# Transposes by DMA in place of a trip through DRAM, and whole tables in place of placed ones, in a spectral filter with a feed-forward layer on one core

## The chip, the cores and the metric

One core of one Trainium2 chip (trn2). The metric is the device time of one execution in microseconds, lower is better. Most executions of a kernel agree within 0.3%. Verdicts compare a kernel with the kernel before on the same chip, in the same rounds.

In the profile lines PE is TensorE's matmuls and PEld its weight loads, DVE is VectorE, ACT ScalarE, POOL GpSimd; SPq and ACTq are the queues from which SyncE and ScalarE issue DMAs; L723 is a line of the kernel. The chain that ended last is the work followed back from the last instruction, at each step to what released it. The granted clock is the share of TensorE's full clock that it was given.

## The reference, cut to what matters

```python
# x: (8, 3008, 256); w_r, w_i: (256, 256); moe_w_in: (256, 2048); moe_w_out: (2048, 256)
X = np.fft.rfft(x, axis=1)
Yr = Xr @ w_r - Xi @ w_i + b_r            # and Yi likewise
Y = soft_threshold(Yr, 0.01) + 1j * soft_threshold(Yi, 0.01)
y = np.fft.irfft(Y, n=3008, axis=1)
h = np.maximum(y.reshape(24064, 256) @ moe_w_in, 0)
out = (s * h * h + b) @ moe_w_out
```

The kernel splits the transform of length 3008 into 94 x 32. A batch goes through four stages: the first transform over 94 points (matrix A_t), the second over 32 (F_t) with the mixing by w, the inverse over 32 (T_t), and the last over 94 (C_t). Then come the two large matrix products, which fill most of TensorE's time. The stages of the next batches are woven into the large products of the present one. The plan counts in slots: one slot is a sixteenth of a tile of the large layer, some 1.08 us.

Of the kernel before, what the change touches and what calls it, by code (L numbers as in the profile page):

```python
# [9 lines left out]
F16 = mybir.dt.float16  # L10
# [4 lines left out]
P = 128  # L15
# [81 lines left out]
def kernel(  # L97
# [26 lines left out]
    F_d = nc.inline_tensor(fwd.astype(np.float16), name="dft_fwd").ap()  # L124
    T_d = nc.inline_tensor(inv.astype(np.float16), name="dft_inv").ap()
# [14 lines left out]
    upool = ctx.enter_context(tc.tile_pool(name="up", bufs=3))  # L140
    uspool = ctx.enter_context(tc.tile_pool(name="usp", bufs=5))
# [3 lines left out]
    vspool = ctx.enter_context(tc.tile_pool(name="vsp", bufs=2))  # L145
# [75 lines left out]
    F_c = uspool.tile([P, NPAIR, 2, N2], F16, name="F_c", tag="us")  # L221
# [6 lines left out]
    T_c = uspool.tile([P, NPAIR, 64], F16, name="T_c", tag="us")  # L228
# [9 lines left out]

    def emit_load_forward():
        nc.sync.dma_start(  # L240
            out=F_c[:, 0:H].rearrange("p q r k -> p q (r k)"), in_=F_d[:, 0:H]
        )
        nc.sync.dma_start(out=sel_t, in_=S_d)

    def emit_load_inverse():
        nc.sync.dma_start(
            out=F_c[:, H:].rearrange("p q r k -> p q (r k)"), in_=F_d[:, H:]
        )
        t_load = nc.sync.dma_start(out=T_c, in_=T_d)
# [22 lines left out]
    F_t = cpool.tile([P, NPAIR, P], F16, name="F_t")  # L272
    nc.vector.memset(F_t, 0.0)
    T_t = cpool.tile([P, NPAIR, P], F16, name="T_t")
    nc.vector.memset(T_t, 0.0)
    F_2 = [uspool.tile([P, H, P], F16, name="F_2", tag="us") for _ in range(2)]
    for f in F_2:
        nc.gpsimd.memset(f, 0.0)
# [21 lines left out]
    def place_f(h):  # L300
        q = slice(h * H, h * H + H)
        for a in range(2):
            r = slice(64 * a, 64 * a + 64)
            nc.scalar.copy(out=blocks(F_t)[r, q, :, a], in_=F_c[r, q])

    def place_f_2(h):

        q = slice(h * H, h * H + H)
        for a in range(2):
            r = slice(64 * a, 64 * a + 64)  # L310
            nc.vector.tensor_scalar_mul(
                out=blocks(F_2[h])[r, :, 0, a], in0=F_c[r, q, 1], scalar1=-1.0
            )
            nc.vector.tensor_copy(out=blocks(F_2[h])[r, :, 1, a], in_=F_c[r, q, 0])

    def place_t(h):
        q = slice(h * H, h * H + H)
        for i in range(4):
            r = slice(32 * i, 32 * i + 32)
            c = 64 * (i % 2)  # L320
            nc.vector.tensor_copy(out=T_t[r, q, c : c + 64], in_=T_c[r, q])
# [28 lines left out]
    def first_batch():  # L350
# [3 lines left out]
        for g in range(N2 // 4):  # L354
# [26 lines left out]
            if c == 2:  # L381
                with tc.issue_after(last_dve.ins):
                    nc.vector.memset(F_c[0:1, H, 0, 0:1], 0.0)
                    nc.vector.memset(T_c[0:1, 0, 0:1], 0.0)
# [4 lines left out]
        with tc.issue_after(last_dve.ins), tc.issue_after(last_act.ins):  # L389
            place_f(0)  # L390
            place_f_2(0)

        gate = nc.gpsimd.tensor_copy(out=w_in_t[0][0:1, 0:1], in_=T_c[0:1, 0, 0:1])
# [9 lines left out]
        g_last = [None]  # L403

        def mix(ec, u):
# [10 lines left out]
            if u % 3 == 1:  # L416
                g_last[0] = nc.scalar.copy(out=g, in_=ps)
                load["act"] += 1.02
            else:
                g_last[0] = nc.vector.tensor_tensor(  # L420
# [47 lines left out]
        for h in range(2):  # L468
            vs[(0, h)] = vspool.tile([96, HW, D], F16, name="vs", tag="vs")

        def turn(ec, k):
            ps = two_banks()
            for j in range(8):
# [4 lines left out]
            h, n = divmod(8 * k, HW)  # L478
            evac(
                vs[(0, h)][:, n : n + 8, ec * P : (ec + 1) * P],  # L480
# [5 lines left out]
        def last_dft(ec, n2):  # L486

            ps = [one_bank(), other_bank()]
            for j in range(8):
                h, k = divmod(n2 + j, HW)  # L490
                nc.tensor.matmul(
                    ps[j // 4][:, (j % 4) * 96 : (j % 4) * 96 + 96],
                    vs[(0, h)][:, k, ec * P : (ec + 1) * P], C_t,
# [8 lines left out]
        more = s1_units(1, True)  # L502
# [7 lines left out]
        for i in range(2 * U + 2):  # L510
# [13 lines left out]
            if i == 0:  # L524
                with tc.issue_after(g_last[0].ins):
                    place_t(0)
            if i == 1:
# [397 lines left out]
```

## The kernel before: the parts that the change touches

```python
def s1_units(b, more_banks=False):                  # first stage of a batch, 16 units
    def unit(i):
        c, j = divmod(2 * i, XCH)
        ps = ...
        nc.tensor.matmul(ps[0:96, :], A_t[0:N1, :], x16[(b, c)][0:N1, j * D : (j + 2) * D], ...)
        evac(u[0:96, j : j + 2, :], ps..., 512)     # ScalarE or VectorE, by a tally
        if j == XCH - 2:                            # four stores to DRAM ...
            nc.sync.dma_start(out=ud[:, c * XCH : (c + 1) * XCH, :], in_=u[0:96])
        if i == N2 // 2 - 1:                        # ... and four loads in the other layout
            for q in range(4):
                t = ...
                nc.sync.dma_start(out=t, in_=uv[:, 6 * q : 6 * q + 6, :])

def inv_unit(i):                                    # inverse over 32 (in s23_units)
    ...
    if i % 2 == 1:                                  # v goes to DRAM, six stores a batch
        nc.sync.dma_start(out=vd[2 * i - 2 : 2 * i + 2]..., in_=v)
    if i == H - 1:                                  # after the last: vs is read back, in two loads
        for h in range(2):
            t = ...
            nc.sync.dma_start(out=t..., in_=vv[:, h * HW * D : (h + 1) * HW * D])

# s4_units: the last transform, matmuls on C_t and vs

for b in range(2, B):                               # s0, s1, s2: first slots of batches b-2, b-1, b
    p = s1 - s0
    schedule(s0 + 40, p - 48, s1_units(b))          # first stage ends 8 slots before s1
    p = s2 - s1
    schedule(s1 + 2, p - 30, s23_units(b))          # vs of batch b is requested near s2 - 28
    schedule(s2 - 14, 12, s4_units(b))              # and read from s2 - 14 on
```

SyncE issues all of these DMAs, and the stores of the output, in the order in which they stand in its instruction stream.

## Time and profile before

| | before |
|---|---|
| median of three runs | 851.42 us (851.32 to 852.76) |
| span of the profiled run | 849.4 us |
| TensorE busy | 835.0 us |
| granted clock of TensorE, mean | 0.997 |
| waits of TensorE for vs | none |

The lines behind it stand in the prediction. One reads them from the top: if TensorE is busy for 98% of the span, a change can win only by giving TensorE less to do, or in the start-up, where TensorE idles.

### The profile page before, as it was taken

The numbers are of one execution on the slowest core, as the hardware profiler recorded it, in microseconds if no ns is written. First come the engines' busy times: TensorE is split into PE (matmuls) and PEld (weight loads), VectorE is DVE, ScalarE is ACT, GpSimd is POOL, SyncE is SP. The second block draws the span as 40 slices with busy tenths as digits, with TensorE's granted clock in tenths as the row PEclk, the third lists the DMA queues.
The fourth block names the chain that finished last, engine by engine and source line by source line (L and its number), as shares of the span: only waits on it lengthen the run. The fifth ranks groups of instructions, "written<-read, shape, count | busy, mean of one in ns | idle before, by whom it ended". The sixth has DMA issues, their size and how long they took to land.

```text
span 849.4 us, 17085 instructions
## 1 busy us (share of the span) xinstructions
PE 835.0 (98%) x6645; PEld 600.5 (71%) x6645; DVE 697.0 (82%) x1027; ACT 643.2 (76%) x856; POOL 46.6 (5%) x72
## 2 busy tenths in 40 slices
PE   8899999999999999999999999999999999999997
PEld 7757777777677766777677776777667777766765
DVE  6898987888888987888878888888977888776674
ACT  5898887787778787787777887787877787766673
POOL 5321000000000000000000000000000000000000
PEclk9999999999999999999999999999999999999999
DMA  7937457324761367324662247613354223411111
GB/s 165 161 104 162 108 148 185 101 76 100 177 186 54 92 159 184 109 78 103 171 177 65 74 106 199 172 40 92 100 156 118 62 79 98 112 33 38 38 44 50
DMA packets 105458, 95.07 MB, mean 112 GB/s; under 512 B 9510, under 2 KB 97578, under 8 KB 104034
## 3 DMA queue, kind: packets, MB, share of 16 engines
q1 hardware_dynamic: 98930, 79.57, 32.6%
q0 software_dynamic: 6448, 14.42, 10.7%
q8 instruction: 52, 0.85, 0.4%
q14 instruction: 28, 0.23, 0.1%
HBM read 52.54 MB, written 46.66 MB: 117 GB/s over the span
## 4 chain that ended last, share of the span: by engine, by line
PE 88%; DVE 4%; ACT 3%; DMA 2%; issue 1%; POOL 0%; SPq 0%; DVEq 0%; ACTq 0%; POOLq 0%
PE psa L832 36%; PE psh L761 36%; PE psf L627 4%; PE psf L562 2%; PE psf L613 2%; PE psf L598 2%; PE psf L657 2%; PE psf L710 2%; ACT rt L768 1%; DVE gt L775 1%; DMA x<-in_x_dram 1%; DMA out_dram<-ost 1%; PE psh L410 1%; ACT yt L160 0%; ACT vs L160 0%
## 5 line engine op out<-in xcount | busy, mean ns | idle before, releaser
L768 ACT ACTIVATE rt<-psh 128x1024 f32<-128x1024 f32 (+2 forms) x384 | 387.1, 1009 | 119.1 <-PE psh L761 117.7
L775 DVE TENSOR_TENSOR gt<-rt 128x1024 f16<-128x1024 f32 (+2 forms) x321 | 384.0, 1199 | 98.1 <-ACT rt L768 97.4
L832 PE MATMUL psa<-w_out_t,gt 128*128 128x256 f16 (+1 forms) x3024 | 454.3, 272 | 0.1
L832 PEld LDWEIGHTS <-gt 128*128 128x128 f16 (+1 forms) x3024 | 300.9, 101 | 187.2 <-issue 1.7
L761 PE MATMUL psh<-yt,w_in 128*128 128x512 f16 (+1 forms) x1344 | 396.7, 378 | 0.3 <-ACT rt L768 0.3
L761 PEld LDWEIGHTS <-w_in 128*128 128x128 f16 x1536 | 142.9, 98 | 27.4 <-issue 2.1
L842 DVE SCALAR_TENSOR_TENSOR ost<-psa,s_bc,bias_bc 128x512 f32<-128x512 f32 (+2 forms) x97 | 71.0, 732 | 8.3 <-PE psa L832 7.1
L772 ACT ACTIVATE gt<-rt 128x1024 f16<-128x1024 f32 (+2 forms) x63 | 66.2, 1050 | 1.0
L632 DVE TENSOR_TENSOR ring<-psf,s 128x512 f16<-128x512 f32 x84 | 57.5, 684 | 3.7 <-PE psf L627 2.9
L160 ACT CAST v<-psf 128x512 f16<-128x512 f32 x78 | 45.3, 582 | 18.7 <-PE psf L657 18.7
L160 ACT CAST xf<-psf 128x512 f16<-128x512 f32 x82 | 47.9, 585 | 10.9 <-PE psf L598 10.8
L160 ACT CAST u<-psf 96x512 f16<-96x512 f32 x77 | 44.5, 580 | 11.0 <-PE psf L562 10.7
L761 PE MATMUL psh<-tail,w_in 128*128 128x512 f16 (+1 forms) x192 | 52.1, 353 | 0.0
L627 PE MATMUL psf<-W_g,xf 128*128 128x256 f16 x336 | 50.4, 273 | 0.0
L160 ACT CAST yt<-psf 128x480 f16<-128x480 f32 (+2 forms) x75 | 38.1, 520 | 13.6 <-PE psf L710 13.6
L189 POOL DMA_DIRECT2D x<-in_x_dram x36 | 18.9, 530 | 429.3 <-PE psf L562 428.0
L562 PE MATMUL psf<-x,A_t 94*96 94x512 f16 x104 | 39.7, 381 | 1.7 <-ACT yt L160 0.5
L638 DVE TENSOR_TENSOR ring<-ring,high 128x512 f16<-128x512 f16 x84 | 35.5, 423 | 2.3
L639 DVE TENSOR_TENSOR ring<-ring 128x512 f16<-128x512 f16 x84 | 35.5, 422 | 1.9
L637 DVE TENSOR_TENSOR ring<-ring,low 128x512 f16<-128x512 f16 x84 | 35.4, 421 | 1.6
L627 PEld LDWEIGHTS <-xf 128*128 128x128 f16 x336 | 32.9, 98 | 3.8
L710 PE MATMUL psf<-C_t,vs 96*128 96x96 f16 x448 | 33.0, 205 | 0.1
(89 smaller groups left out, 501.9 us busy)
## 6 DMA issues: line engine op xcount, KB each, us to landing
out_dram<-ost SPq DMA_DIRECT2D x152, 128.0 KB
ud<-u SPq DMA_DIRECT2D x28, 384.0 KB
us<-ud SPq DMA_DIRECT2D x28, 384.0 KB
vd<-v SPq DMA_DIRECT2D x42, 256.0 KB
vs<-vd SPq DMA_DIRECT2D x14, 768.0 KB
x<-in_x_dram POOLq DMA_DIRECT2D x28, 376.0 KB, 5.9
ring<-ring SPq DMA_DIRECT2D x280, 32.0 KB
out_dram<-ost SPq DMA_DIRECT2D x16, 120.0 KB
```

What stands on the lines that cost most here:

```text
L160: return None, nc.scalar.copy(out=dst, in_=src)
L562: nc.tensor.matmul(ps[0:96, :], A_t[0:N1, :], x16[(b, c)][0:N1, j * D : (j + 2) * D], start=True, stop=True,)
L627: nc.tensor.matmul(ps[:, r, :], xt[:, 2 - r, dc], W_g[:, dc, r], start=(dc == 0), stop=(dc == DC - 1),)
L632: nc.vector.tensor_tensor(out=t, in0=ps, in1=hold[i // 2][:, i % 2].unsqueeze(1).to_broadcast([P, 2, D]), op=ALU.add,)
L638: nc.vector.tensor_tensor(out=m, in0=m, in1=high, op=ALU.min)
L710: nc.tensor.matmul(ps[:, j * 96 : (j + 1) * 96], vs[(b, h)][:, k, ec * P : (ec + 1) * P], C_t, start=True, stop=True,)
L761: nc.tensor.matmul(o, w_in_t[dc][:, mc * P : (mc + 1) * P], r, start=(dc == 0), stop=(dc == DC - 1),)
L768: nc.scalar.activation(out=rt[:, :, 0:w], in_=ps[:, :, 0:w], func=AF.Relu)
L772: nc.scalar.activation(out=gt[:, :, 0:w], in_=rt[:, :, 0:w], func=AF.Square)
L775: nc.vector.tensor_tensor(out=gt[:, :, 0:w], in0=rt[:, :, 0:w], in1=rt[:, :, 0:w], op=ALU.mult)
L832: nc.tensor.matmul(ps[0:size, h, :], gts[(ti, mc // 2)][:, mc % 2, sub * size : (sub + 1) * size], w_out_t[:, mc, :], start=(mc == 0), sto ...
L842: nc.vector.scalar_tensor_tensor(out=ost[0:size, 0:k], in0=ps[0:size, 0:k], scalar=s_bc[0:size], in1=bias_bc[0:size, 0:k], op0=ALU.mult, o ...
```

## The change

The intent: the first stage's result for batches 2 to 7 no longer goes through DRAM to change its layout. TensorE computes it with the two operands exchanged, so that it lies with the 256 features on partitions, and two transposing DMAs a batch turn it, SBUF to SBUF. The stage is moved 20 slots ahead of where it ended. Besides, the inverse table and the second half of the forward tables are loaded whole, where they were spread on the chip by VectorE and ScalarE.

```diff
+        def unit_late(i):
+            ...
+            for j in range(4):
+                nc.tensor.matmul(
+                    ps[:, j * 96 : j * 96 + 96], x16[(b, c)][0:N1, lo : lo + P],
+                    A_t[0:N1, :], start=True, stop=True,
+                )
+            evac(u[:, dc, :, 4 * g : 4 * g + 4], ps[:, 0:384]..., 384)
+            if i == N2 // 2 - 1:
+                us[b] = uspool.tile([P, NPAIR, D], F16, name="us", tag="us")
+                for dc in range(DC):
+                    nc.sync.dma_start(
+                        out=us[b][:, :, dc * P : (dc + 1) * P],
+                        in_=u[:, dc].rearrange("p k n -> p (k n)"),
+                        transpose=True,
+                    )
... (batch 1 keeps the trip through DRAM)
-        schedule(s0 + 40, p - 48, s1_units(b))
+        lead = 40 if b == 2 else 28
+        schedule(s0 + lead, p - lead - 28, s1_units(b))
...
-        t_load = nc.sync.dma_start(out=T_c, in_=T_d)
+        nc.sync.dma_start(out=T_t[:, 0:H], in_=t_d[:, 0:H])
+        nc.sync.dma_start(out=F_t[:, H:], in_=f_d)
+        nc.sync.dma_start(out=F_2[1], in_=f_2_d)
+        t_load = nc.sync.dma_start(out=T_t[:, H:], in_=t_d[:, H:])
... (place_t and the second calls of place_f and place_f_2 go; us, u and vs get single buffers, each of a whole batch)
```

More of the change, by code (lines that the diff above doesn't have):

```diff
@@ L123 @@
     A_d = nc.inline_tensor(first.astype(np.float16), name="dft_first").ap()
-    F_d = nc.inline_tensor(fwd.astype(np.float16), name="dft_fwd").ap()
-    T_d = nc.inline_tensor(inv.astype(np.float16), name="dft_inv").ap()
+    F_d = nc.inline_tensor(fwd[:, 0:H].astype(np.float16), name="dft_fwd").ap()
+    f_all = np.zeros((P, NPAIR, 2, 2, N2))
+    t_all = np.zeros((P, NPAIR, 2, 64))
+    for i in range(4):
+        r = slice(32 * i, 32 * i + 32)
+        f_all[r, :, :, i // 2] = fwd.reshape(P, NPAIR, 2, N2)[r]
+        t_all[r, :, i % 2] = inv[r]
+    f_2 = np.stack([-f_all[:, H:, 1], f_all[:, H:, 0]], axis=2)
+    f_d, f_2_d, t_d = (
+        nc.inline_tensor(t.reshape(P, -1, P).astype(np.float16), name=name).ap()
+        for t, name in ((f_all[:, H:], "fwd_rest"), (f_2, "fwd_rest_i"), (t_all, "dft_inv"))
+    )
     C_d = nc.inline_tensor(last.astype(np.float16), name="dft_last").ap()
@@ L139 @@
     xpool = ctx.enter_context(tc.tile_pool(name="xp", bufs=4))
-    upool = ctx.enter_context(tc.tile_pool(name="up", bufs=3))
-    uspool = ctx.enter_context(tc.tile_pool(name="usp", bufs=5))
+    upool = ctx.enter_context(tc.tile_pool(name="up", bufs=1))
+    uspool = ctx.enter_context(tc.tile_pool(name="usp", bufs=1))
     xfpool = ctx.enter_context(tc.tile_pool(name="xfp", bufs=4))
@@ L144 @@
     vpool = ctx.enter_context(tc.tile_pool(name="vp", bufs=3))
-    vspool = ctx.enter_context(tc.tile_pool(name="vsp", bufs=2))
+    vspool = ctx.enter_context(tc.tile_pool(name="vsp", bufs=1))
     ypool = ctx.enter_context(tc.tile_pool(name="yp", bufs=2))
@@ L220 @@
             nc.sync.dma_start(out=b_g[r : r + 1, i], in_=bv.unsqueeze(0))
-    F_c = uspool.tile([P, NPAIR, 2, N2], F16, name="F_c", tag="us")
+    first_c = uspool.tile([P, 5, H * 64], F16, name="first_c", tag="us")
+    F_c = first_c[:, 0].rearrange("p (q r k) -> p q r k", q=H, r=2)
+    F_2 = [
+        first_c[:, 1 + 2 * i : 3 + 2 * i].rearrange("p s (q k) -> p (s q) k", k=P)
+        for i in range(2)
+    ]
     b_h = cpool.tile([P, D], F16, name="b_h")
@@ L227 @@
     sel_t = cpool.tile([P, P], F16, name="sel_t")
-    T_c = uspool.tile([P, NPAIR, 64], F16, name="T_c", tag="us")
     eye_t = cpool.tile([P, P], F16, name="eye_t")
@@ L237 @@
     bb_bc = cpool.tile([P, 1], F32, name="bb_bc")
+    F_t = cpool.tile([P, NPAIR, P], F16, name="F_t")
+    T_t = cpool.tile([P, NPAIR, P], F16, name="T_t")
     def emit_load_forward():
         nc.sync.dma_start(
-            out=F_c[:, 0:H].rearrange("p q r k -> p q (r k)"), in_=F_d[:, 0:H]
+            out=F_c.rearrange("p q r k -> p q (r k)"), in_=F_d
         )
@@ L245, in emit_load_inverse @@
     def emit_load_inverse():
-        nc.sync.dma_start(
-            out=F_c[:, H:].rearrange("p q r k -> p q (r k)"), in_=F_d[:, H:]
-        )
-        t_load = nc.sync.dma_start(out=T_c, in_=T_d)
+        nc.sync.dma_start(out=T_t[:, 0:H], in_=t_d[:, 0:H])
+        nc.sync.dma_start(out=F_t[:, H:], in_=f_d)
+        nc.sync.dma_start(out=F_2[1], in_=f_2_d)
+        t_load = nc.sync.dma_start(out=T_t[:, H:], in_=t_d[:, H:])
         with tc.issue_after(t_load.ins):
@@ L271 @@
     nc.vector.memset(neg_lam, -LAM)
-    F_t = cpool.tile([P, NPAIR, P], F16, name="F_t")
-    nc.vector.memset(F_t, 0.0)
-    T_t = cpool.tile([P, NPAIR, P], F16, name="T_t")
-    nc.vector.memset(T_t, 0.0)
-    F_2 = [uspool.tile([P, H, P], F16, name="F_2", tag="us") for _ in range(2)]
-    for f in F_2:
-        nc.gpsimd.memset(f, 0.0)
+    nc.vector.memset(F_t[:, 0:H], 0.0)
+    nc.gpsimd.memset(F_2[0], 0.0)
     def make_bounds():
@@ L298, in place_w, with place_f, place_f_2 @@
             nc.scalar.copy(out=W_t[:, :, i], in_=w_st[i])
-    def place_f(h):
-        q = slice(h * H, h * H + H)
+    def place_f():
         for a in range(2):
             r = slice(64 * a, 64 * a + 64)
-            nc.scalar.copy(out=blocks(F_t)[r, q, :, a], in_=F_c[r, q])
-    def place_f_2(h):
-        q = slice(h * H, h * H + H)
+            nc.scalar.copy(out=blocks(F_t)[r, 0:H, :, a], in_=F_c[r])
+    def place_f_2():
         for a in range(2):
@@ L311, in place_f_2 @@
             nc.vector.tensor_scalar_mul(
-                out=blocks(F_2[h])[r, :, 0, a], in0=F_c[r, q, 1], scalar1=-1.0
+                out=blocks(F_2[0])[r, :, 0, a], in0=F_c[r, :, 1], scalar1=-1.0
             )
-            nc.vector.tensor_copy(out=blocks(F_2[h])[r, :, 1, a], in_=F_c[r, q, 0])
-    def place_t(h):
-        q = slice(h * H, h * H + H)
-        for i in range(4):
-            r = slice(32 * i, 32 * i + 32)
-            c = 64 * (i % 2)
-            nc.vector.tensor_copy(out=T_t[r, q, c : c + 64], in_=T_c[r, q])
+            nc.vector.tensor_copy(out=blocks(F_2[0])[r, :, 1, a], in_=F_c[r, :, 0])
     w_sum = cpool.tile([P, D], F16, name="w_sum")
@@ L382, in first_batch @@
                 with tc.issue_after(last_dve.ins):
-                    nc.vector.memset(F_c[0:1, H, 0, 0:1], 0.0)
-                    nc.vector.memset(T_c[0:1, 0, 0:1], 0.0)
+                    for t in (T_t[:, 0:H], F_t[:, H:], F_2[1], T_t[:, H:]):
+                        nc.vector.memset(t[0:1, 0, 0:1], 0.0)
                 emit_load_inverse()
@@ L389, in first_batch @@
         with tc.issue_after(last_dve.ins), tc.issue_after(last_act.ins):
-            place_f(0)
-            place_f_2(0)
-        gate = nc.gpsimd.tensor_copy(out=w_in_t[0][0:1, 0:1], in_=T_c[0:1, 0, 0:1])
+            place_f()
+            place_f_2()
+        gate = nc.gpsimd.tensor_copy(out=w_in_t[0][0:1, 0:1], in_=F_t[0:1, H, 0:1])
         with tc.issue_after(gate.ins):
@@ L402, in first_batch @@
         zt = {}
-        g_last = [None]
         def mix(ec, u):
@@ L416, in mix @@
             if u % 3 == 1:
-                g_last[0] = nc.scalar.copy(out=g, in_=ps)
+                nc.scalar.copy(out=g, in_=ps)
                 load["act"] += 1.02
             else:
-                g_last[0] = nc.vector.tensor_tensor(
+                nc.vector.tensor_tensor(
                     out=g, in0=ps,
@@ L466, in inv_dft @@
             )
-        for h in range(2):
-            vs[(0, h)] = vspool.tile([96, HW, D], F16, name="vs", tag="vs")
+        vs[0] = vspool.tile([P, N2, D], F16, name="vs", tag="vs")
         def turn(ec, k):
@@ L477, in turn @@
                 )
-            h, n = divmod(8 * k, HW)
             evac(
-                vs[(0, h)][:, n : n + 8, ec * P : (ec + 1) * P],
+                vs[0][0:96, 8 * k : 8 * k + 8, ec * P : (ec + 1) * P],
                 ps[0:96].rearrange("p h (j e) -> p (h j) e", e=P), 1024,
@@ L489, in last_dft @@
             for j in range(8):
-                h, k = divmod(n2 + j, HW)
                 nc.tensor.matmul(
                     ps[j // 4][:, (j % 4) * 96 : (j % 4) * 96 + 96],
-                    vs[(0, h)][:, k, ec * P : (ec + 1) * P], C_t,
+                    vs[0][0:96, n2 + j, ec * P : (ec + 1) * P], C_t,
                     start=True, stop=True,
@@ L500, in last_dft @@
                 )
-        more = s1_units(1, True)
+        more = s1_units(1, late=False)
         def some(n):
@@ L523, in first_batch @@
                 some(3)
-            if i == 0:
-                with tc.issue_after(g_last[0].ins):
-                    place_t(0)
-            if i == 1:
-                with tc.issue_after(g_last[0].ins):
-                    place_f(1)
-            if i == 2:
-                with tc.issue_after(g_last[0].ins):
-                    place_f_2(1)
-            if i == 3:
-                with tc.issue_after(g_last[0].ins):
-                    place_t(1)
             if i == 9:
@@ L549, in first_batch, with s1_units @@
         return more
-    def s1_units(b, more_banks=False):
-        ud = dpool.tile([96, N2, D], F16, name="ud", tag="ud")
+    def s1_units(b, late=True):
         hold = {}
+        def unit_late(i):
+            g, dc = divmod(i, DC)
+            if i == 0:
+                hold["u"] = upool.tile([P, DC, 96, N2], F16, name="u", tag="u")
+            u = hold["u"]
+            c, h = divmod(g, 2)
+            ps = one_bank()
+            for j in range(4):
+                lo = (4 * h + j) * D + dc * P
+                nc.tensor.matmul(
+                    ps[:, j * 96 : j * 96 + 96], x16[(b, c)][0:N1, lo : lo + P],
+                    A_t[0:N1, :], start=True, stop=True,
+                )
+            evac(
+                u[:, dc, :, 4 * g : 4 * g + 4],
+                ps[:, 0:384].rearrange("p (n k) -> p k n", k=96), 384,
+            )
+            if i == N2 // 2 - 1:
[5 more added lines that the diff above has]
+                        transpose=True,
+                    )
         def unit(i):
             c, j = divmod(2 * i, XCH)
-            if j == 0:
-                hold["u"] = upool.tile([P, XCH, D], F16, name="u", tag="u")
-            ps = other_bank() if more_banks and i % 2 else one_bank()
+            if i == 0:
+                hold["u"] = upool.tile([P, 3, XCH, D], F16, name="u1", tag="u")
+                hold["ud"] = dpool.tile([96, N2, D], F16, name="ud", tag="ud")
+            ps = other_bank() if i % 2 else one_bank()
             nc.tensor.matmul(
@@ L565, in unit @@
             )
-            u = hold["u"]
+            u, ud = hold["u"][:, c % 3], hold["ud"]
             evac(u[0:96, j : j + 2, :], ps[0:96, :].rearrange("p (j d) -> p j d", j=2), 512)
             if j == XCH - 2:
-                nc.sync.dma_start(
-                    out=ud[:, c * XCH : (c + 1) * XCH, :], in_=u[0:96]
-                )
+                nc.sync.dma_start(out=ud[:, c * XCH : (c + 1) * XCH, :], in_=u[0:96])
             if i == N2 // 2 - 1:
                 uv = ud.rearrange("k n d -> (k n) d").rearrange("(q p) d -> p q d", p=P)
+                us[b] = uspool.tile([P, NPAIR, D], F16, name="us", tag="us")
                 for q in range(4):
-                    t = uspool.tile([P, 6, D], F16, name="us", tag="us")
-                    nc.sync.dma_start(out=t, in_=uv[:, 6 * q : 6 * q + 6, :])
-                    us[(b, q)] = t
+                    nc.sync.dma_start(
+                        out=us[b][:, 6 * q : 6 * q + 6], in_=uv[:, 6 * q : 6 * q + 6, :]
+                    )
+        if late:
+            return [lambda i=i: unit_late(i) for i in range(N2 // 2)]
         return [lambda i=i: unit(i) for i in range(N2 // 2)]
@@ L593, in fwd_unit @@
             ps = bank.rearrange("p (r c j k) -> p r c j k", r=2, c=DC, j=2)
-            t = us[(b, i // 3)]
             for j in range(2):
-                q = (2 * i + j) % 6
                 for dc in range(DC):
                     nc.tensor.matmul(
-                        ps[:, :, dc, j, :], t[:, q, dc * P : (dc + 1) * P],
+                        ps[:, :, dc, j, :], us[b][:, 2 * i + j, dc * P : (dc + 1) * P],
                         F_t[:, 2 * i + j, :], start=True, stop=True,
@@ L670, in inv_unit @@
                 vv = vd.rearrange("q (k n) e -> (q k) (n e)", n=N2)
+                t = vs[b] = vspool.tile([P, N2, D], F16, name="vs", tag="vs")
                 for h in range(2):
-                    t = vspool.tile([96, HW, D], F16, name="vs", tag="vs")
                     nc.sync.dma_start(
-                        out=t.rearrange("k n e -> k (n e)"),
+                        out=t[0:96, h * HW : h * HW + HW].rearrange("k n e -> k (n e)"),
                         in_=vv[:, h * HW * D : (h + 1) * HW * D],
                     )
-                    vs[(b, h)] = t
         units = []
@@ L708, in unit @@
             for j in range(w):
-                h, k = divmod(n2 + j, HW)
                 nc.tensor.matmul(
                     ps[:, j * 96 : (j + 1) * 96],
-                    vs[(b, h)][:, k, ec * P : (ec + 1) * P], C_t,
+                    vs[b][0:96, n2 + j, ec * P : (ec + 1) * P], C_t,
                     start=True, stop=True,
@@ L861, in load_x_2 @@
     def load_x_2():
-        emit_load_x(2, us[(1, 3)][0:1, 0, 0:1])
+        emit_load_x(2, us[1][0:1, NPAIR - 1, 0:1])
     mark = {}
```

## The prediction

> **What bounds the kernel now.** I read the page from the top: busy shares first, then the chain that ended last, then the stretches of time, and only then single lines. Here are the busy shares and the chain by engine.
>
> ```profile
> PE 835.0 (98%) x6645; PEld 600.5 (71%) x6645; DVE 697.0 (82%) x1027; ACT 643.2 (76%) x856; POOL 46.6 (5%) x72
> ...
> PE 88%; DVE 4%; ACT 3%; DMA 2%; issue 1%; POOL 0%; SPq 0%; DVEq 0%; ACTq 0%; POOLq 0%
> ```
>
> TensorE is busy for 835.0 of 849.4 us and makes up 88% of the chain. All that it idles is 14.4 us. The view of stretches says where (us, then busy time of PE, PEld, DVE, ACT, POOL, the granted clock, the DMA share, GB/s):
>
> ```profile
> 15.00:25.00 10.00, 8.07 (x91) 6.67 (x89) 9.28 (x20) 8.34 (x13) 4.61 (x8) 1.00 0.80 168
> 25.00:35.00 10.00, 9.27 (x118) 7.88 (x116) 8.16 (x11) 7.65 (x13) 2.06 (x3) 1.00 1.15 207
> 35.00:45.00 10.00, 8.55 (x112) 6.93 (x110) 9.01 (x15) 8.81 (x16) 8.36 (x9) 1.00 0.43 59
> ...
> 320.00:423.00 103.00, 102.79 (x799) 72.61 (x798) 86.63 (x131) 80.05 (x108) 3.82 (x6) 1.00 0.49 126
> 423.00:526.00 103.00, 102.85 (x801) 72.76 (x800) 86.81 (x129) 80.01 (x107) 3.28 (x5) 1.00 0.47 121
> ```
>
> Two regimes follow. From about 52 us on, a batch takes 103 us, of which TensorE works over 102.7, at full clock. VectorE has 16% and ScalarE 22% to spare there, and the DMA engines are half busy. In that part only two things count: TensorE's own work, and any new wait that makes it stop. In the first 52 us TensorE has gaps, and VectorE and ScalarE, at 80 to 93%, set the pace. Only there can saved copies buy time.
>
> **What the Trainium skill says.**
> 1. "TensorE: Matmul & The Clock Gate", section "Back-to-back issue gap": a warm matmul follows the one before after N/2.4 + 2.5 ns, so 42.5 ns for 96 columns and 215.8 for 512. The trace agrees (below). The same section gives about 81 ns for a stream of weight load and matmul pairs at 128 columns. The trace doesn't show that: in the start-up such pairs (L441) begin at 27.46, 27.51, 27.57, 27.62 us, 55 ns apart.
> 2. "DMA: Bandwidth & Descriptors", section "Latency and other measured facts": a transposing DMA was measured at 261 GB/s with a non-contiguous middle dimension, 350 to 400 in the contiguous case. The kernel before has none, so the trace says nothing of it.
> 3. "VectorE: DVE Perf Modes", section "The three transpose paths": 1309 ns for one 128x128 tile by DMA, which is 25 GB/s if such tiles simply follow one another. It is ten times away from the second point, and my main uncertainty.
> 4. "DMA: Bandwidth & Descriptors", section "Queues, rings and completion order": each DMA engine takes the descriptors of a ring in order. So what SyncE issues after a transpose stands behind it. The trace before can't confirm it.
>
> **The change part by part.**
>
> (a) The first stage on TensorE, batches 2 to 7. Before: 16 matmuls a batch with A_t as weights and 512 moving columns. After: x is the weight, A_t moves, so 64 matmuls of 96 columns. The second form already runs in the start-up, for batch 0. From the timeline there:
>
> ```profile
> 12.55 0.34 PE L361 MATMUL psh<-A_t,x 94*128 94x96 f16 x4
> 12.72 0.33 PE L361 MATMUL psf<-A_t,x 94*128 94x96 f16 x4
> 12.89 0.44 PE L202 MATMUL psa<-ones 128*128 128x128 f16 x5
> ```
>
> Eight matmuls from 12.55 to 12.89 us: 42.5 ns each, weight loads hidden. (The duration in the second column contains the pipeline's tail.) The old form in the steady part runs from 412.07 us to the next matmul at 412.29: 0.22 us. Per batch 64 x 42.5 ns = 2.72 us takes the place of 16 x 0.216 = 3.46 us. That is 0.74 less, and for six batches **-4.4 us**. It lies on the bound engine, so it counts in full. I take 4.2, since short groups between other matmuls may hide their weight loads a little less well.
>
> (b) Its evictions: 16 a batch either way, 96x512 before and 128x384 after. The groups by shape:
>
> ```profile
> L160 ACT CAST u<-psf 96x512 f16<-96x512 f32 x77 | 44.5, 580 | 11.0 <-PE psf L562 10.7
> L164 DVE CAST ut<-psf 128x384 f16<-128x384 f32 x8 | 4.5, 558 | 5.5 <-PE psf L361 5.4
> L160 ACT CAST ut<-psh 128x384 f16<-128x384 f32 x8 | 3.8, 479 | 7.8 <-PE psh L361 7.7
> ```
>
> About 0.1 us each on either engine (VectorE's old one took 682 ns), 1.6 to 2 us a batch. Neither engine bounds there, so it gives 0.
>
> (c) The start-up. Gone are eight T_t copies on VectorE (8 x 360 ns = 2.9 us), the second half of F_2 (2 x 303 + 2 x 247 ns = 1.1 us) and two F_t copies on ScalarE (2 x 829 ns = 1.66 us). Of these, six pieces lie on the chain (start, duration, what):
>
> ```profile
> 17.66 0.83 ACT F_t L304
> ...
> 19.10 0.83 ACT F_t L304
> ...
> 24.20 0.26 DVE T_t L321
> ...
> 24.46 0.35 DVE T_t L321
> ...
> 24.83 0.22 DVE T_t L321
> 25.20 0.36 DVE T_t L321
> ```
>
> Together 1.66 + 1.19 = 2.85 us. Other work of the same pipeline will be the next limit, so I count **-2.3 us**. The price is 1.57 MB of tables in place of 0.59 MB. At the 168 to 207 GB/s of these stretches the extra 0.98 MB is an estimated 5 to 6 us of DMA time. The first inverse matmul ran at 20.53 us and the first use of the second forward half at 27.46 us, the loads start at 13.1 us in the order of need, and the weights behind them are first needed at 51.65 us. I expect no wait of over 0.5 us.
>
> (d) The trip through DRAM. Per batch a write and a read of 1.57 MB give way to two transposes of 0.79 MB each (128 x 24 x 128 values of 2 bytes), SBUF to SBUF. The DMA engines are half idle, so the saved traffic buys nothing by itself. What matters is the place of the transposes. The first stage now ends some 28 slots (of 1.08 us) before the batch boundary, not 8. The order of SyncE's instructions in the changed kernel shows both transposes among the last stores of v to vd, just ahead of the two loads of vs. Those loads have a deadline, the last transform of the preceding batch. Before, without transposes (start, duration; SyncE's issues, then the first consumer on TensorE):
>
> ```profile
> 415.59 0.37 SPq L666 DMA_DIRECT2D vd<-v  x1
> 418.34 0.80 SPq L673 DMA_DIRECT2D vs<-vd  x2
> ...
> 429.45 0.59 PE L710 MATMUL psf<-C_t,vs 96*128 96x96 f16 x10
> ```
>
> From the issue of vs to its first use are 11.1 us. The DMA engines then move 238 to 281 GB/s, so the first half (0.79 MB, 3 us, plus about 2 us of latency) is there after some 5 us. The slack is about 6 us. The transposes can start about 3 us ahead of the last vd store. So a pair that takes up to **about 9 us** (175 GB/s or more) stays hidden. At 261 GB/s the pair takes 6.0 us: hidden, **0 us**. As for the forward transform that reads the transposed data, it comes some 16 slots after the last transform's start, at about 447 us here, over 30 us after the transposes' issue: hidden in nearly any case.
>
> Sum: 851.4 - 4.2 - 2.3 = 844.9. I add 0.6 for a chance of small stalls: **845.5 us**.
>
> **The rivals.**
> - A wait on vs takes the place of nothing that was there: the transposes are slower than 175 GB/s and hold up the vd stores and vs loads behind them. For: the authors keep the old trip for batch 1, where time is short, and moved the stage 20 slots ahead, as one does for something slow; each written piece is short. Against: the same authors chose the place, and would have seen a wait. A pair of 12 us costs about 3 us x 6 = 18, so some 863 us; one of 16 us costs 7 x 6 = 42, so 887. At the 1309 ns of the third point, 48 tiles in a row take 63 us, and six times 54 us would give over 1,160 us. I hold that for nearly excluded.
> - SyncE is held long by issuing a transpose, and the stores of out behind it come late. Three buffers of ost, one used every 8.7 us, bear a delay of over 15 us; so about 0 unless the hold is that long.
> - VectorE or ScalarE becomes the bound: no, both lose work.
> - The start-up gains nothing, as the larger tables delay the loads of x and weights: then 847 to 849 us. TensorE in the start-up lacks mainly VectorE and ScalarE results, which speaks against it.
>
> **Range and chances.** Without stalls, 842 to 848.5 us. That has some 70%. Small stalls of 1 to 3 us a batch lead to 849 to 865 (some 14%), longer ones beyond (some 15%). A gain of over 2% (below 834.4) would need 17 us, more than all of TensorE's idle time: only if TensorE's work fell by more than (a). The range is 839 to 864, a little open at the top. Chances: faster 0.03, within 2% 0.80, slower 0.17.
>
> **What would show it.** (a) TensorE's busy time falls to about 831, and groups of four 96-column matmuls in the steady part start the next instruction after 0.17 us. (c) The first matmul of the large layer (L761, 51.65 us before) starts 2 to 3 us sooner. (d) No idle time of TensorE before the reads of vs, and the stretches of one batch last about 102 us instead of 103. The prediction is wrong if the matmuls on C_t and vs, or those on us, show idle time that a DMA ended: then the speed of the transposes is the step that failed. If TensorE's busy time doesn't fall, step (a) did.

## The result, and the profile after

The changed kernel takes 899.64 us (median of four runs, 898.49 to 901.27), before 852.09 us in the same rounds. The ratio is 1.056 (95% interval 1.054 to 1.058): slower by 5.6%, and far outside the predicted range. Ratios here are the mean time of one kernel's runs over that of the other's of the same rounds, so not quite the ratio of the medians. Executions over 1.5% slower than the fastest of the same kernel are left out of the means.

The busy shares and the chain by engine, from the page of the changed kernel:

```profile
PE 844.7 (94%) x6933; PEld 610.5 (68%) x6933; DVE 687.4 (76%) x1011; ACT 639.1 (71%) x859; POOL 45.3 (5%) x71
...
PE 78%; DMA 7%; DVE 7%; ACT 4%; issue 2%; SPq 1%; POOL 0%; DVEq 0%; ACTq 0%; POOLq 0%
```

TensorE's busy time and its idle time both moved the wrong way: 9.7 us more busy time, though the change gives it less work, and 54.8 us of idle time in place of 14.4. DMAs now make up 7% of the chain, before 2%. The list of TensorE's waits (line, what ended the wait, us in total, times, longest) says which one:

```profile
PE psf L723 <- DMA vs<-vd: 39.2, 6, 12.1
```

Six waits, one for each batch that has a transpose ahead of it, for the loads of vs. Here is SyncE's stream around one of them, then the first matmul that reads vs (timelines of the changed kernel: start, duration, queue or engine, line, operation). Compare it with the three lines of before in part (d) of the prediction.

```profile
445.20 3.67 SPq L566 DMA_TRANSPOSE us<-u  x1
448.99 1.26 SPq L807 DMA_DIRECT2D out_dram<-ost  x2
450.35 5.85 SPq L566 DMA_TRANSPOSE us<-u  x1
456.67 0.38 SPq L681 DMA_DIRECT2D vd<-v  x1
...
459.43 0.81 SPq L688 DMA_DIRECT2D vs<-vd  x2
...
465.50 0.98 PE L723 MATMUL psf<-C_t,vs 96*128 96x96 f16 x10 [4.68 <-DMA vs<-vd]
```

TensorE was ready for vs at 465.50 - 4.68 = 460.8 us. Set this to zero. The transposes are issued at -15.6 and -10.4 and hold SyncE's stream for 3.7 and 5.9 us, against 0.4 us for a plain store. The last vd store, due at about -14 as before, comes at -4.1. The load of vs has to wait for it, goes out at -1.4 instead of -11.1, and has 6 us of its own still to go. The load itself moves its data about as fast as before (209 to 262 GB/s from 460 to 466 us in the stretches below, 238 to 281 in the prediction's working); it is late. Nor does the last vd store take longer in itself: in four of the six batches the vs load follows its issue after 2.5 to 3.7 us, before after 2.5 to 5.5. What is late there is the issue of that store, behind the two holds of SyncE's stream. In the other two batches, where TensorE waits longest (8.2 and 12.1 us), 11.4 and 9.9 us pass between the two.

There is a second loss. The view of stretches over the same wait (the last three columns are the granted clock, the DMA share and GB/s):

```profile
460.00:462.00 2.00, 0.81 (x6) 0.39 (x4) 1.01 (x1) 1.02 (x1) 0.00 (x0) 1.00 0.82 209
462.00:464.00 2.00, 0.00 (x0) 0.00 (x0) 0.00 (x0) 0.00 (x0) 0.00 (x0) 0.78 1.00 262
464.00:466.00 2.00, 0.50 (x7) 0.51 (x8) 0.00 (x0) 0.00 (x0) 0.00 (x0) 0.50 1.05 258
...
468.00:470.00 2.00, 2.00 (x12) 1.26 (x11) 0.00 (x0) 1.08 (x2) 0.00 (x0) 0.51 0.21 67
470.00:472.00 2.00, 2.00 (x23) 1.44 (x22) 1.56 (x2) 0.97 (x3) 0.00 (x0) 1.00 0.00 0
```

TensorE stops at 460.8. Its clock falls to half at about 463.1 (worked out from the mean of 0.78 over 462 to 464) and stays there until about 470, 4.5 us after the work resumes: 12 to 13 instructions in 2 us in place of 23. The Trainium skill, "TensorE: Matmul & The Clock Gate", section "What's actually happening", says that after an idle window of about 3.4 us the clock is halved, until a window of work has passed. The trace agrees that a stop halves the clock for some time after it; here the fall came 2.3 us after the stop, sooner than a whole window. The shortest of the six waits, 2.8 us, left the clock at 1.00. Length alone does not decide: a wait of 3.5 us in e1 (from 554.7 us) left it at 1.00, one of 2.2 us in e7 (from 457.5 us) was followed by 0.50. In all these runs every wait of 3.9 us or more in the steady part was followed by a stretch at half clock.

### The profile page after: what moved, and what is told of

The parts are those of the page before. It is cut to its first block, busy times and chain, and to the rows that moved or that the text cites. A ratio compares the mean times of both kernels' runs of the same rounds, so it can differ in the third digit from the quotient of the medians.

```text
span 899.5 us, 17579 instructions
## 1 busy us (share of the span) xinstructions
PE 844.7 (94%) x6933; PEld 610.5 (68%) x6933; DVE 687.4 (76%) x1011; ACT 639.1 (71%) x859; POOL 45.3 (5%) x71
## 3 DMA queue, kind: packets, MB, share of 16 engines
q0 software_dynamic: 6448, 14.42, 10.5%
## 4 chain that ended last, share of the span: by engine, by line
PE 78%; DMA 7%; DVE 7%; ACT 4%; issue 2%; SPq 1%; POOL 0%; DVEq 0%; ACTq 0%; POOLq 0%
PE psa L845 32%; PE psh L774 32%; DMA vs<-vd 4%; PE psf L642 4%; PE psf L723 3%; DVE gt L788 2%; PE psf L628 2%; PE psf L613 2%; PE psf L555 2%; PE psf L672 2%; ACT rt L781 2%; DMA vd<-v 1%; SPq L566 1%; DVE ring L647 1%; DMA x<-in_x_dram 1%
## 5 line engine op out<-in xcount | busy, mean ns | idle before, releaser
L774 PE MATMUL psh<-yt,w_in 128*128 128x512 f16 (+1 forms) x1344 | 400.8, 381 | 0.3 <-ACT rt L781 0.3
L774 PEld LDWEIGHTS <-w_in 128*128 128x128 f16 x1536 | 138.4, 99 | 15.6 <-issue 1.3
L855 DVE SCALAR_TENSOR_TENSOR ost<-psa,s_bc,bias_bc 128x512 f32<-128x512 f32 (+2 forms) x97 | 71.0, 732 | 11.5 <-PE psa L845 11.2
L723 PE MATMUL psf<-C_t,vs 96*128 96x96 f16 x448 | 37.2, 221 | 39.6 <-DMA vs<-vd 39.2
L171 ACT CAST yt<-psf 128x480 f16<-128x480 f32 (+2 forms) x69 | 35.3, 524 | 52.8 <-PE psf L723 52.8
L175 DVE CAST yt<-psf 128x480 f16<-128x480 f32 (+2 forms) x37 | 22.3, 602 | 63.1 <-PE psf L723 62.8
L723 PEld LDWEIGHTS <-vs 96*128 96x128 f16 x448 | 31.6, 106 | 44.6 <-DMA vs<-vd 40.9
L171 ACT CAST xf<-psf 128x512 f16<-128x512 f32 x80 | 46.8, 586 | 10.6 <-PE psf L613 10.5
L774 PE MATMUL psh<-tail,w_in 128*128 128x512 f16 (+1 forms) x192 | 54.1, 364 | 0.0
L171 ACT CAST u<-psf 128x384 f16<-128x384 f32 (+1 forms) x93 | 45.6, 492 | 10.4 <-PE psf L555 9.1
L200 POOL DMA_DIRECT2D x<-in_x_dram x36 | 18.7, 526 | 363.7 <-PE psf L555 362.5
```

What stands on the lines that cost most here:

```text
L171: return None, nc.scalar.copy(out=dst, in_=src)
L723: nc.tensor.matmul(ps[:, j * 96 : (j + 1) * 96], vs[b][0:96, n2 + j, ec * P : (ec + 1) * P], C_t, start=True, stop=True,)
L774: nc.tensor.matmul(o, w_in_t[dc][:, mc * P : (mc + 1) * P], r, start=(dc == 0), stop=(dc == DC - 1),)
L855: nc.vector.scalar_tensor_tensor(out=ost[0:size, 0:k], in0=ps[0:size, 0:k], scalar=s_bc[0:size], in1=bias_bc[0:size, 0:k], op0=ALU.mult, o ...
```

## The experiments

Theory A: the transposes stand ahead of the last vd stores and the vs loads, and delay them, so the order is the cause. Rivals: (B) other parts of the change (single buffers, larger tables, the stage's place among other work) make the waits; (C) the transposes need so much of the DMA engines that any place hurts; (D) the halved clock is a loss of its own.

To compare orders I read from the timelines, for every batch that has transposes, when the last vd store and the first vs load are issued, counted from the moment at which TensorE is ready for vs. The medians over the six batches (for the kernels without transposes, the same six):

| kernel | last vd store | vs load | waits for vs, us | median time, us | before in the same rounds, us | ratio |
|---|---|---|---|---|---|---|
| before | -13.9 | -10.7 | 0 | 851.42 | | |
| changed | -3.9 | 0.0 | 39.2 | 899.64 | 852.09 | 1.056 |
| e1 plain copies | -11.4 | -2.7 | 18.7 | 877.25 | 852.90 | 1.029 |
| e2 tables only | -13.9 | -10.7 | 0 | 849.36 | 851.41 | 0.997 |
| e3 stage later | -13.3 | -9.7 | 0 | 846.73 | 852.90 | 0.993 |
| e4 stage earlier | -11.5 | -7.3 | 1.3 | 854.16 | 852.90 | 1.003 |
| e5 vd, vs by ScalarE | -9.1 | -1.3 | 41.6 | 914.18 | 852.90 | 1.074 |
| e6 idle matmuls | - | - | 11.8 | 893.19 | 851.41 | 1.049 |
| e7 second transpose 10 slots later | -10.3 | -2.9 | 30.4 | 888.88 | 851.41 | 1.042 |
| e12 second behind vs | -10.2 | -4.3 | 22.2 | 877.26 | 851.63 | 1.028 |
| e13 both behind vs | -12.8 | -6.4 | 0.6 | 849.92 | 851.63 | 0.998 |
| e9 stage later, again | -13.3 | -9.9 | 0 | 846.57 | 851.63 | 0.994 |
| e10 later still | -13.4 | -8.8 | 0.5 | 860.33 | 851.63 | 1.010 |

(e6's idle matmuls shift the zero, so its times of issue aren't comparable. The waits are those of the profiled run, the times are medians of all runs.)

### e13: only the order

Nothing moves but the two transposes, which are ordered behind the loads of vs.

```diff
+        def behind_vs(u, dcs):
+            with tc.issue_after(vs_load[b - 1].ins):
+                for dc in dcs:
+                    transpose(u, dc)
...
+        plan.setdefault(s1 - 18, []).append(lambda b=b: second[b]())   # both transposes
```

> The changed kernel, stage in its place, only that both transposes are ordered behind the loads of vs on SyncE: nothing else is moved. If order is the whole cause, waits for vs vanish and the time equals that of the later stage, 844 to 850 us. If the place of the first stage itself matters (its matmuls and evictions among those of the preceding batch), it stays over 855 us.

849.92 us, ratio 0.998 (0.996 to 0.999). SyncE's stream and the first read of vs:

```profile
415.21 0.37 SPq L690 DMA_DIRECT2D vd<-v  x1
421.10 0.81 SPq L697 DMA_DIRECT2D vs<-vd  x2
...
423.37 12.13 SPq L575 DMA_TRANSPOSE us<-u  x2
...
427.76 0.59 PE L732 MATMUL psf<-C_t,vs 96*128 96x96 f16 x10
```

The last vd store is back at -12.6, vs at -6.7, and TensorE reads it without a wait. The transposes hold SyncE for 12.1 us, and only output stores stand behind them. TensorE is busy for 831.9 us in this run:

```profile
PE 831.9 (98%) x6933; PEld 604.5 (71%) x6933; DVE 688.1 (81%) x1011; ACT 637.6 (75%) x859; POOL 46.4 (5%) x71
```

The order accounts for the whole loss: the profiled spans differ by 899.5 - 848.4 = 51.1 us, TensorE's waits for vs by 39.2 - 0.6 = 38.6, its busy time by 844.7 - 831.9 = 12.8, and 38.6 + 12.8 = 51.4. Rivals B and C fall as causes of this loss: single buffers, tables and the stage's place are all still there, and so are the transposes. What is left is small and not explained: e13 takes 3.35 us more than e9, the stage later, in the same rounds.

### e12 and e7: one of the two ahead

e7 emits the second transpose 10 slots later in the plan; e12 orders it behind the loads of vs as in e13, with the first left in place.

> The changed kernel with its first transpose where it was and the second one 10 slots later, behind the loads of vs. Theory A: with half of the work ahead of vd and vs the last vd store goes out at about -12 us before the first read of vs instead of -3 to -6, and the waits for vs fall from 39 us to under 6 in total: 844 to 853 us. Rival C (any transposing ahead of vs is harmful): over 870 us.

> The changed kernel, stage in its place, first transpose in its place, but the second one ordered behind the loads of vs (the earlier split failed in that the scheduler kept it ahead of them). If the order alone is the cause, one transpose of some 5 to 6 us uses up the slack of about 6 us and no more: last vd store at -10 to -14 us before the first read of vs, vs issued at -6 to -9, waits under 6 us in total, 845 to 856 us. If vs is as late as with both ahead, over 880 us.

e7 missed its aim. The scheduler, which orders each engine's stream by its own estimate, kept the second transpose ahead of the vs load; only the last vd store got past it (-10.3). That wasn't enough: the waits came to 30.4 us, 888.88 us in all. e12 has the intended order, and its result lies between my two figures: waits of 22.2 us, 877.26 us. Four of the batches wait 0 to 2.4 us, and two wait 8.2 and 9.2, those in which the first transpose comes late or holds SyncE for 10.1 us instead of 3.6. With two, one and no transpose ahead, the waits are 39.2, 22.2 and 0.6 us. That fits theory A. My expectation was wrong in that one transpose does not always stay within the slack.

### e1: plain copies in the place of the transposes

```diff
-                        in_=u[:, dc].rearrange("p k n -> p (k n)"),
-                        transpose=True,
+                        in_=u[:, dc].rearrange("p k n -> p (k n)").rearrange("p (q k) -> p q k", k=P),
```

The same bytes between the same tiles, in the same order; the result is wrong.

> The changed kernel with each of the 12 transposes replaced by a plain copy of the same bytes between the same two tiles (the result is wrong on purpose). Theory A, the transposes' own cost on SyncE and on the DMA engines makes vd and vs late: the waits of TensorE for vs (39.2 us in six in the changed kernel) shrink to under 3 us, SyncE's issue of a copy takes about 0.5 us instead of 3.6 to 10.6, the time is 843 to 848 us. Rival B, the stage's new place, the fewer buffers or the larger tables make the waits: the time stays above 885 us with waits for vs of over 30 us.

Neither: 877.25 us, waits of 18.7 us. SyncE's stream around one wait, then the first read of vs:

```profile
432.51 0.66 SPq L566 DMA_DIRECT2D us<-u  x1
...
437.06 0.65 SPq L566 DMA_DIRECT2D us<-u  x1
438.16 5.14 SPq L680 DMA_DIRECT2D vd<-v  x1
...
446.03 0.81 SPq L687 DMA_DIRECT2D vs<-vd  x2
...
451.69 0.51 PE L722 MATMUL psf<-C_t,vs 96*128 96x96 f16 x8 [2.69 <-DMA vs<-vd]
```

SyncE issues a copy in 0.65 to 1.4 us, so the issue of the vd store begins at -11.4, but the vs load comes only at -2.7: behind the 1.57 MB of copies the vd store needs some 8.7 us, against 2.7 us in the last batch of that run, which has no copy ahead. In part the hold has only moved: the issue of the vd store itself takes 3.3 to 6.6 us in the six batches, 0.4 in the last. So about half of the waits (18.7 of 39.2) comes from moving 1.57 MB at this spot in pieces of 128 values, even untransposed, and the other half from its being transposed. That reading rests on one kernel of each kind.

### e5: vd and vs on another queue

```diff
-                nc.sync.dma_start(out=vd[...]..., in_=v)
+                nc.scalar.dma_start(out=vd[...]..., in_=v)
... (and the two loads of vs)
```

> The changed kernel with the vd stores and the vs loads of all batches issued by ScalarE instead of SyncE; the transposes stay on SyncE in their place. It separates the two halves of theory A. If SyncE's hold and the order in its own rings are what delays vs (A1), the waits for vs fall under 10 us in total and the time is 846 to 858 us. If the transposes delay others through the shared DMA engines (A2), vs still lands late, waits stay over 25 us, over 875 us.

914.18 us, waits of 41.6 us. ScalarE's queue around one wait:

```profile
444.21 0.37 ACTq L681 DMA_DIRECT2D vd<-v  x1
...
452.21 0.89 ACTq L688 DMA_DIRECT2D vs<-vd  x2
```

Free of SyncE's stream and rings, the last vd store still takes about 8.0 us until vs can follow (3.8 to 9.6 in the six batches). In the last batch of the same run, without a transpose in flight, it takes 2.5 (-8.8 to -6.3). By its numbers the run meets the second alternative (A2): here another queue did not get past a transpose in flight. It is no clean separation of the two halves of theory A: in this kernel the last inverse matmul itself lies only 10.5 us ahead of the read instead of 14.2, and ScalarE waits for vd's landing in its own stream, where it does no other work for 6.1 us. What share SyncE's hold has of its own stays open, and so does why a transpose holds SyncE so long.

### e3, e4, e10, e9: where the pair fits

```diff
-        schedule(s0 + lead, p - lead - 28, s1_units(b))
+        schedule(s0 + lead, p - lead - 18, s1_units(b))     # e3, e9; e10 has 13
...
+        lead = 34 if b == 2 else 20                         # e4
+        schedule(s0 + lead, p - lead - 40, s1_units(b))
```

> The changed kernel with the first stage of batches 2 to 7 ending 18 slots before the boundary instead of 28, so that the transposes are issued some 10 us after the loads of vs and not ahead of them. Theory A (they are costly only because vd and vs stand behind them, on SyncE and in the rings): waits for vs under 3 us, no wait for us, 843 to 850 us. Rival C (they need so many DMA engine-microseconds that any place hurts): the wait moves to the forward transform (matmuls on us) or stays, over 865 us.

> The changed kernel with the first stage of batches 2 to 7 some 8 slots earlier at its start and ending 40 slots before the boundary, so that the transposes are issued some 12 us ahead of where they were, before the last stores of vd. Theory A: they are done before the last vd store is due, waits for vs fall from 39 to under 8 us in total, 845 to 858 us. Rival C: over 870 us.

> The kernel of the later placed transposes again, on another chip with more rounds, as the candidate that beats both: 844 to 849 us, a ratio to before of 0.990 to 0.996, and no wait for vs.

> The later stage once more, ending 13 slots before the boundary instead of 18: the transposes have some 16 us until the forward transform reads them. With a pair taking 10 to 16 us beside other loads that is the edge: 844 to 852 us, and if it is too late, waits of TensorE for us (not vs) of 1 to 4 us a batch, up to 870 us.

Ending 18 slots before the boundary, the stage has its transposes issued behind the vs load, and there is time until the forward transform. Two chips give 0.993 (0.990 to 0.996) and 0.9945 (0.9925 to 0.9965): this kernel, correct, beats the changed one clearly and the kernel before by a little. In e9 one batch still waited 1.5 us for us. The page of e3 has

```profile
PE 830.0 (98%) x6933; PEld 605.0 (72%) x6933; DVE 685.9 (81%) x1009; ACT 637.5 (76%) x861; POOL 47.0 (6%) x71
```

Ending at 13, the pair is late on the other side. TensorE waits for us, in four batches:

```profile
PE psf L613 <- DMA us<-u: 9.1, 4, 4.3
```

and the time is 860.33 us (the profiled run, the fastest of six, took 856.63). Ending at 40 it takes 854.16: waits for vs have nearly gone (1.3 us), but TensorE's busy time is 835.5 us rather than 830.0. What costs that I did not follow up.

### e8: how long a pair takes

e4 with two one-element reads of the result by GpSimd, one look only (854.43 us, state unknown).

> The earlier placed transposes with two one-element GpSimd reads of their result, which show when each has landed, in a stretch where the DMA engines have little else to do. If a transpose moves its 0.79 MB at the 261 GB/s that I took, each lands some 5 us after its issue (3 us and 2 us of latency) and the pair within 8. If its own issue on SyncE bounds it, the pair takes 9 to 12 us. Time within 5 us of the earlier run.

```profile
405.76 9.52 SPq L567 DMA_TRANSPOSE us<-u  x2
...
413.71 0.40 POOL L573 COPY probe<-us 1x1 f16<-1x1 f16 x1 [7.23 <-DMA us<-u]
417.26 0.18 POOL L573 COPY probe<-us 1x1 f16<-1x1 f16 x1 [3.16 <-DMA us<-u]
```

The first has landed 8.0 us after the issue, the pair after 11.5: 1.57 MB / 11.5 us = 137 GB/s from issue to landing, with one load of x beside it, where I had taken 261 GB/s for the pair's occupancy (6.0 us; some 8 with latency). In the other batches where the two are issued back to back the pair takes 9.5 to 12.7 us. By its numbers this is the second alternative of the expectation. The stretches between issue and landing (columns as before, the last is GB/s) show where the time goes:

```profile
410.00:412.00 2.00, 2.00 (x15) 1.27 (x13) 1.93 (x5) 1.91 (x3) 0.00 (x0) 1.00 1.19 259
412.00:414.00 2.00, 2.00 (x16) 1.39 (x15) 1.90 (x5) 1.61 (x3) 0.29 (x1) 1.00 1.20 251
414.00:416.00 2.00, 2.00 (x17) 1.41 (x15) 1.90 (x6) 2.00 (x3) 0.11 (x1) 1.00 1.15 218
```

Once the data move, their rate is 218 to 259 GB/s, all traffic counted, not far under the 261 that I took. What I left out is the time before that, some 4 us from the first issue to 410 us, in which a load of x also runs.

### e6: the clock

```diff
+                if b < B - 1:
+                    busy = one_bank()
+                    for _ in range(80):
+                        nc.tensor.matmul(busy[:, 0:P], ones, ones, start=True, stop=True)
```

> The changed kernel with 80 idle matmuls of 128 columns (4.5 us) ahead of the first transform that reads vs, in batches 1 to 6. They fill waits of 2.8 to 12.1 us that are there anyway. If TensorE's halved clock after each wait is a loss of its own (theory D, some 14 us in the sum), the granted clock goes up from 0.975 towards 0.99 and the time falls by 4 to 14 us to 886 to 896. If the clock doesn't matter, the time stays within 2 us of the changed kernel or grows by up to 5.

893.19 us, 6.4 us less than the changed kernel's median (each in its own rounds; the ratios are 1.049 and 1.056). The added matmuls, an estimated 6 x 80 x 55 ns = 26.4 us (the spacing of such matmuls in the start-up), replace 39.2 - 11.8 = 27.4 us of waits, so by themselves they change nothing. The granted clock rose from 0.975 to 0.994. The clock is thus a loss of its own, and not all of it was undone.

### e2: tables only

Every batch goes through DRAM again, at the old places (late units out, the old call of schedule back). The single buffers stay.

> The changed kernel with all batches through DRAM again, in the old places; what is left of the change is the loading of whole tables (and the single buffers). If that part does what the start-up of the changed kernel's trace suggests (first matmul of the large layer at 47.9 instead of 49.6 us), the time is 1.5 to 2 us under before, 849 to 851 us, TensorE busy about 835 us, no wait for vs. Rival B (the tables or the fewer buffers cost something later): 855 us or more.

849.36 us against 851.41, 2.05 us less, without waits for vs. The tables do what they were meant to do, and the single buffers cost nothing that shows.

## Why the prediction was wrong, point by point

- **What bounds the kernel**: right. TensorE has no slack, so a new wait counts in full, and the prediction named this one as its first rival. (One slip: ScalarE was busy for 7.65 of 10 us in the second stretch of the start-up, 77% and not "80 to 93%".)
- **(a) TensorE's work**: right in mechanism and nearly in size. In the changed kernel a group of four goes from 432.67 us to the next matmul at 432.84, 0.17 us:

```profile
432.67 0.34 PE L555 MATMUL psf<-A_t,x 94*128 94x96 f16 x4
432.84 0.60 PE L774 MATMUL psh<-yt,w_in 128*128 128x512 f16 x2
```

  TensorE's busy time, where no wait disturbs it, is 830.0 us (e3) against 833.5 with tables only (e2): 3.5 us less, against 4.2 predicted.
- **(b) Evictions**: gave nothing, as said.
- **(c) Start-up**: predicted 2.3 us; e2 measured 2.05, and the first matmul of the large layer starts at 47.9 us instead of 49.6. I had named 51.65 as its start before; that was the first longer piece in the chain, not the first matmul.
- **(d) The place of the transposes**: this step failed. It said: "At 261 GB/s the pair takes 6.0 us: hidden, **0 us**", after allowing "up to **about 9 us**". Three terms were off. The pair takes 9.5 to 12.7 us even in quiet surroundings (e8). It does not start 3 us ahead as a whole: the first transpose starts at about -16, 2 us ahead of the last vd store's due time, but the second follows at -10.4, after the vd stores should have gone, and SyncE's stream is held 3.6 to 10.6 us by each. I had held such a hold harmless because I looked only at the output stores behind it, not at vd and vs. The last vd store so went out at -3.9 instead of -13.9, and these 10 us are nearly the whole delay of the vs load (10.7 us). The prediction had said that in such a case the speed of the transposes is what failed. That is so only in part: the rate of the data was not far under the assumed one (e8), the hold of SyncE and the late second transpose were not in the sum at all. (The 2 us of latency in that sum were assumed without a source; the lines shown there bear them out roughly, with 2.75 us from the issue of the last vd store, 0.26 MB, to the load that waits for it.)
- **The size of the first rival**: it gave 887 us for a pair of 16 us, that is waits of 42 us. From the first transpose to the vs load are indeed about 16 us, and the waits came to 39.2. That the two agree is in part luck: put in the pair's own time of 9.5 to 12.7 us (e8), and the same rule gives waits of 3 to 22 us. What it lacked besides is the clock, 12.8 us of slower matmuls. Its chance, some 15%, was too low: two figures that lay ten times apart should have weighed more against a slack of 6 us than the thought that the authors would have seen a wait.
- **The sum without waits**: 844.9 us was predicted, 6.5 under before. The same operations in a place where they harm nothing give 846.6 to 846.7 us, 5.1 and 6.2 under before in their rounds. The failed step is the only large one.

## What to carry to other kernels

A DMA that is off the critical path can still decide the time by where it stands in its queue: before moving one, list what is issued behind it, with the deadline of each, and measure the new transfer's time rather than take it from a figure. Put the transfer with the loose deadline behind the one with the tight deadline; here the same two transposes cost 50 us in front of a load and nothing that shows behind it (e13); with the stage later as well they gain some 3 to 4 us beyond what the tables gain. On a kernel whose TensorE never rests, count a wait of several us at more than its length: every wait of 3.9 us or more in these runs was followed by a stretch at half clock, and of the shorter ones some.

## What the Trainium skill lacked or had wrong

- "DMA: Bandwidth & Descriptors" (latency and other measured facts): its 261 GB/s for a transposing DMA fits the rate while the data of the pair move (218 to 259 GB/s of all traffic in e8), but it is no figure for how long a pair of 0.79 MB each takes, SBUF to SBUF. From issue to landing that was 11.5 us, 137 GB/s.
- "VectorE: DVE Perf Modes" (the three transpose paths): 1309 ns for a 128x128 tile must not be multiplied. 48 such tiles in two instructions landed in 11.5 us, 0.24 us each.
- No page has in us how long the issuing engine's stream of a trn2 is held by one transpose of such a size; the nearest is a cycle count for "previous generations", in a part on trn3. It was 3.5 to 14.2 us on SyncE in these runs, against 0.65 to 1.4 us for a plain copy of the same bytes (e1), after which, however, the next store held SyncE for 3.3 to 6.6 us.
- "DMA: Bandwidth & Descriptors" (issuing engines are not separate DMA queues) says that DMAs of all issuing engines run on the same 16 DMA engines. No page has a number for what e5 shows, how long a store on ScalarE's queue is delayed by transposes in flight on SyncE's: 3.8 to 9.6 us from its issue until the load that waits for it goes out, against 2.5 without.
- "TensorE: Matmul & The Clock Gate" (back-to-back issue gap): N/2.4 + 2.5, which the page gives for isolated matmuls, holds here in streams too (42.5 ns at 96 columns), but the 81 ns for pairs of weight load and matmul at 128 columns doesn't; here it is 55 ns.
